# A filter reload queued behind the first stores, and a turned class taken ahead of the products

## The chip, the core and the metric

The kernel runs on one core of a Trainium2 chip. The core has a matrix engine (TensorE, PE in the profile), a vector engine (VectorE, DVE), a scalar engine for pointwise functions (ScalarE, ACT), a general one (GpSimd, POOL) and a sync engine (SyncE, SP). Each follows its own list of instructions in order, and engines wait for one another by semaphores. SP's list consists here of transfers (DMAs): it waits until one may go, issues it and goes on; 16 DMA engines then move the bytes. TensorE writes into a memory of its own, PSUM, which VectorE and ScalarE read out ("evict").

The metric is the device time of one execution in microseconds (us), lower being better.

## What is computed

A global filter over a sequence, then a two-layer network on every token:

```python
X = np.fft.rfft(x, axis=1)                 # x: 8 x 3008 x 256
Y = X * (filt_r + 1j * filt_i)[None]       # filters: 1505 x 256
y = np.fft.irfft(Y, n=x.shape[1], axis=1)
t = y.reshape(8 * 3008, 256)
h = t @ w_in                               # 256 -> 2048
g = h * (1.0 / (1.0 + np.exp(-beta * h)))
out = g @ w_out                            # 2048 -> 256
```

## The kernel before

**The filter of one batch** is a Fourier transform of length 3008 = 47 x 64 made of matrix products, in stages:

- s1 (L613): 16 units, each one product of the input tile xg with table t1 (L619) and one eviction of 96x512 into a tile a1. Four units fill one a1 tile, and the fourth also issues the tile's store to DRAM (d1), L624. Batch 1 takes the odd units' evictions to ScalarE.
- a2_read (L626): four loads (L631) bring d1 back in another layout. The first waits for all four stores.
- s23 (L634): 15 units. Unit i below 12 makes two products (L641) and multiplies them with the filter: VectorE takes p_t from frr (L652) and q_t from fri in two halves (L653, L656), and GpSimd adds them (L657). From unit 3 on there is also the inverse product of unit i - 3 (L667), evicted by ScalarE to z, and every third of these issues a store (L672).
- zz_read and s4 (L674, L682): z is read back and the last product gives y.

The real filter in **frr** is laid out for batches 1 to 7 in 24 slots k. It comes by load_filter (L127): for each third of the slots (8 of 24) four loads of 256 KB, lower (L131) and upper (L134) rows for each of the two halves of the partitions. Slots 8 to 23 of frr hold pieces of w_out until GpSimd has scaled them into wout_sb (L151).

**Batch 0** goes another way, before the network starts, and keeps its result z_t in the chip. It is brought into y in four groups g of eight classes each: turn_z (L532), two per group, is eight transposes (L536) with one eviction by VectorE into a tile zz; last_z (L564), four per group, is four products (L544) and one eviction into y. Group 0 is done before the network starts; groups 1 to 3 run inside it. The evictions of last_z are ScalarE's for groups 1 and 3 and VectorE's for group 2.

**The network** (L812) runs over 47 blocks of 512 tokens and in each over 16 slices of the hidden layer: 752 steps. Step s makes the slice's two hidden products (L825) into hps and ScalarE's activation to gT (L834), then the units that a plan has for this step, then the four output products (L860) of the slice two steps back. After a block's last slice the two halves are evicted to ost tiles and stored (L786, L800).

**The plan** is made by place(a, z, units): it spreads units evenly over steps a to z, and moves one on to the next step where a step already has `per` units. Units of a step stand in the order in which place put them there. The same order holds on every engine, SP's queue among them.

**Pools.** PSUM pool fpsum has three buffers for all these units (L619, L641, L667, L536 and L544); hpsum has two for hps, opsum three for acc. apool has three a1 tiles, the first of which group 0 of batch 0 uses as its zz; so batch 1's a1 tiles 0 and 3 are the same buffer. zzpool has four zz tiles, ostp three ost tiles. A tile's new owner waits until the readers of the old one are done.

**Marks.** L506 is a store of 512 bytes from the last piece of batch 1's input. It stands on SP's queue, so that nothing behind it goes out before that input has landed.

In the listing the lines that the change touches are L520 to L522 (the loads of the first third), uf (L731) and the calls of place from L754 to L768.

Of the kernel before, what the change touches and what calls it, by code (L numbers as in the profile page):

```python
# [24 lines left out]
M = 64  # L25
H = M // 2
NK = 24
J = 32
KG = 6
NG = NK // KG  # L30
JG = 8
# [6 lines left out]
def kernel(  # L38
# [10 lines left out]
    nc = tc.nc  # L49
# [38 lines left out]
    frr = consts.tile([P, NK, D], F32, name="frr", tag="frr")  # L88
# [38 lines left out]
    def load_filter(f_sb, filt, at, k0, n, eng):  # L127
        lo = AP(filt.tensor, filt.offset + k0 * D, [[N1 * D, H], [1, n * D]])
        hi = AP(filt.tensor, filt.offset + (N1 - k0) * D, [[N1 * D, H], [-D, n], [1, D]])
        return [  # L130
            lambda: eng.dma_start(  # L131
                f_sb[at : at + H, k0 : k0 + n, :].rearrange("p k d -> p (k d)"), lo
            ),
            lambda: eng.dma_start(f_sb[at + H : at + M, k0 : k0 + n, :], hi),  # L134
        ]
# [13 lines left out]
    def scale_wout(i):  # L149
        fs = slice(i * WG, (i + 1) * WG)  # L150
        nc.gpsimd.tensor_tensor(  # L151
            wout_sb[:, fs, :],
            staged(i),
            rbeta_sb[:, fs].unsqueeze(2).broadcast_to([P, WG, D]),
            ALU.mult,
        )
# [360 lines left out]

    for i in range(4):
        scale_wout(i)
    for at in (0, M):  # L520
        for go in load_filter(frr, filt_r, at, 0, JG, nc.sync):
            go()  # L522

    ys = {}
    ys[0] = ypool.tile([P, NDC, NK * P], BF16, name="y", tag="y")
# [4 lines left out]
    def turn_z(g, i, on_act=False):  # L530
        if g not in zz0:
            zz0[g] = zzpool.tile([KP, JG, D], BF16, name="zz", tag="zz")  # L532
        pz = fpsum.tile([P, 4, D], BF16, name="pz", tag="f")
        for e in range(4):
            for dc in range(NDC):
                nc.tensor.transpose(  # L536
                    pz[:KP, e, dc * P : (dc + 1) * P], z_t[:, dc, JG * g + 4 * i + e, :], ident[:]
                )
        evac(zz0[g][:, 4 * i : 4 * i + 4, :], pz[:KP], on_act)
# [24 lines left out]
    def last_z(g, i, on_act, own=None):  # L564
        jq, dc = divmod(i, NDC)
        c = g * JG // JC + jq
        yv = ys[0][:, dc, c * CLS : (c + 1) * CLS].rearrange("p (n j) -> p n j", j=JC)

        n0 = NP if jq == 0 else (TB - CLS) // JC
        return last4(zz0[g], t4b, JC * jq, dc, yv, on_act, own, n0)  # L570
# [55 lines left out]
    def a2_read(b):  # L626
        s = st[b]
        s["a2"] = []
        for h in range(NG):
            t = a2pool.tile([P, KG, D], BF16, name="a2", tag="a2")  # L630
            nc.sync.dma_start(t[:], s["d1c"][:, h * KG : (h + 1) * KG, :])  # L631
            s["a2"].append(t)
# [41 lines left out]
    def zz_read(b):  # L674
        s = st[b]
        s["zz"] = []
        for h in range(NJG):
            t = zzpool.tile([KP, JG, D], BF16, name="zz", tag="zz")
            nc.sync.dma_start(t[:], s["d2r"][:, h * JG : (h + 1) * JG, :])
            s["zz"].append(t)  # L680
# [15 lines left out]
    def place(a, z, units, clear=False, per=1):  # L696
        last_at = a
        for n, go in enumerate(units):
            at = a + (z - a) * n / max(1, len(units) - 1)
            at = max(int(at), last_at)  # L700
            if clear and (at % NFB < 2 or at % NFB > 13):
                at += (2 - at) % NFB
            while len(plan.get(at, ())) >= per:
                at += 1
            plan.setdefault(at, []).append(go)
            last_at = at
        return last_at

    def u1(b, act=False):
        def unit(i):  # L710
            def go():
                if i == 0:
                    start(b)
                s1(b, i, act and i % 2 == 1)

            return go

        return [unit(i) for i in range(J // 2)]

    def u23(b):  # L720
        return [lambda i=i: s23(b, i) for i in range(NK // 2 + VLAG)]

    def u4(b, act=False):
        return [lambda i=i: s4(b, i, act and i % 2 == 1) for i in range(J // 2)]

    def uz(g, act=False):
        return [lambda i=i: turn_z(g, i) for i in range(2)] + [
            lambda i=i: last_z(g, i, act) for i in range(2 * NDC)
        ]

    def uf():  # L731
        return [
            go
            for k0 in range(JG, NK, JG)
            for at in (0, M)
            for go in load_filter(frr, filt_r, at, k0, JG, nc.sync)
        ]


    def ut(n):  # L740
        return [
            lambda k=k: nc.vector.tensor_scalar_mul(
                t3[M:P, k : k + NK // n], t3b[M:P, k : k + NK // n], -1.0
            )
            for k in range(0, NK, NK // n)
        ]
# [6 lines left out]

    place(2, 14, uz(1, True))  # L754
    place(15, 29, uz(2))
    place(34, 58, uz(3, True))

    first_step = [(S * b // TB) * NFB for b in range(B + 1)]
    if B > 1:
        units = u1(1, True)  # L760
        place(3, 8, units[: J // 4], per=2)
        at = place(9, 14, units[J // 4 :], per=2)
        place(at + 1, at + 1, [lambda: a2_read(1)] + uf(), per=9)
        place(14, 20, ut(4), per=2)
        at = place(25, 56, u23(1), per=2)
        assert at < 60
        place(60, 60, [lambda: zz_read(1)], per=9)
        place(67, 79, u4(1), per=2)  # L768
    if B > 2:
        place(36, 36, ux(2), per=9)  # L770
        at = place(50, 66, u1(2, True), per=3)
        assert at < 74
        place(74, 74, [lambda: a2_read(2)], per=9)
    for b in range(2, B):
        a = first_step[b - 1]
# [36 lines left out]
    for s in range(len(steps) + LAG):  # L812
# [28 lines left out]
        if s >= LAG:  # L841
# [16 lines left out]
            per = acc[0].shape[1]  # L858
# [48 lines left out]
```

## Time and profile before

| what | before |
| --- | --- |
| time, median of 5 runs (lowest to highest) | 789.58 us (788.66 to 792.14) |
| the profiled execution | 789.58 us, with a span of 787.5 us from the first to the last instruction |
| granted TensorE clock | 1.00 |
| first hidden product of the network | at 35.75 us |
| TensorE busy, 40 to 50 us / 50 to 60 us / 60 to 70 us | 9.89 / 8.25 / 9.95 us |
| TensorE busy, 70 to 80 us / 80 to 90 us / 90 to 100 us | 9.63 / 9.32 / 9.95 us |
| VectorE busy, 60 to 70 us / 70 to 80 us / 80 to 90 us | 6.00 / 9.71 / 9.72 us |
| d<-a, stores of a1 (L624): count, KB, median us to landing | 28, 384, 3.8 |
| a<-d, reads of a2 (L631) | 28, 384, 4.9 |
| frr<-in_filt_r_dram, the filter's loads (L131, L134) | 12, 256, 7.0 |

A row of a timeline has: start in us from the span's start, duration in us, engine, line, operation, output<-input, number; and in brackets how long the engine stood idle before it and who released it. "SPq" is SP issuing a transfer, so its duration is that of the issue and not that of the transfer. Rows of like instructions are merged, so that a row's duration can contain waits between its members. The chain of waits is followed back from the end of the execution: each step is the thing that released the next.

### The profile page before, as it was taken

The page shows a single profiled execution, that of the slowest core. Times are in us where ns is not written, and L with a number is a line of the kernel's source. Part 1 is how long each engine was busy: PE and PEld are TensorE (multiplying, and loading weights), DVE is VectorE, ACT ScalarE, POOL GpSimd, SP SyncE. Part 2 cuts the span into 40 slices and gives each one's busy share as a digit, 9 for nine tenths or more (in the row PEclk, how much of TensorE's full clock was granted, in tenths as well). Part 3 has the DMA queues.
Part 4 walks back from the last instruction along what each step waited for, and adds up shares of the span by engine and source line. Part 5 has one row for each costly group of instructions (what it writes and reads, how often), then busy time and mean ns, then how long its engine had stood idle before and what let it go on. Part 6 is the DMA issues. An engine that isn't in the chain of part 4 may idle for free.

```text
span 787.5 us, 15454 instructions
## 1 busy us (share of the span) xinstructions
PE 771.1 (98%) x6015; PEld 547.8 (70%) x6111; DVE 394.1 (50%) x645; ACT 597.2 (76%) x922; POOL 144.5 (18%) x143
## 2 busy tenths in 40 slices
PE   8999999999999999999999999999999999999997
PEld 5767667766777667876668766686667766776665
DVE  8837835646436564465635746267462761500101
ACT  6977886886678866788677876778767788677776
POOL 8522500420014200231002310024000340000000
PEclk9999999999999999999999999999999999999999
DMA  9978674517801187012850238412370214100101
GB/s 192 250 172 227 161 202 134 126 67 199 223 27 67 52 211 206 28 67 96 200 172 27 95 106 184 151 56 85 112 206 28 75 67 127 49 33 28 55 27 54
DMA packets 84185, 91.46 MB, mean 116 GB/s; under 512 B 4498, under 2 KB 74276, under 8 KB 83154
## 3 DMA queue, kind: packets, MB, share of 16 engines
q1 hardware_dynamic: 81008, 73.95, 30.5%
q0 software_dynamic: 2816, 16.26, 10.6%
q8 instruction: 48, 0.79, 0.4%
q10 hardware_dynamic: 288, 0.26, 0.1%
q14 instruction: 25, 0.20, 0.1%
HBM read 57.16 MB, written 46.66 MB: 132 GB/s over the span
## 4 chain that ended last, share of the span: by engine, by line
PE 90%; DVE 4%; DMA 3%; issue 2%; ACT 1%; DVEq 0%; SPq 0%; ACTq 0%
PE acc L860 41%; PE hps L825 37%; PE ps L619 3%; PE ps L544 3%; PE ps L641 2%; PE ps L667 2%; DMA frr<-in_filt_r_dram 1%; PE pw L187 1%; DVE ost L109 1%; DMA out_dram<-ost 1%; DVE qb_t L444 1%; DMA d<-a 1%; DVE a_t L109 0%; DVE pb_t L444 0%; DVE q_t L656 0%
## 5 line engine op out<-in xcount | busy, mean ns | idle before, releaser
L834 ACT ACTIVATE gT<-hps,beta_sb 128x512 bf16<-128x512 f32 x752 | 516.2, 687 | 175.2 <-PE hps L825 146.9
L860 PE MATMUL acc<-wout_sb,gT 128*128 128x256 bf16 x3008 | 455.1, 272 | 3.8 <-ACT ost L107 0.2
L825 PE MATMUL hps<-y,win_sb 128*128 128x512 bf16 (+8 forms) x1636 | 427.4, 350 | 0.4 <-ACT gT L834 0.3
L860 PEld LDWEIGHTS <-gT 128*128 128x128 bf16 x3008 | 285.4, 98 | 132.3 <-issue 4.3
L825 PEld LDWEIGHTS <-win_sb 128*128 128x128 bf16 x1730 | 164.9, 98 | 24.8 <-issue 0.6
L657 POOL TENSOR_TENSOR v_t<-p_t,q_t 128x512 bf16<-128x512 f32 x84 | 106.6, 1269 | 393.7 <-DVE q_t L656 390.8
L109 DVE COPY ost<-acc 128x512 f32<-128x512 f32 (+1 forms) x88 | 56.2, 678 | 193.6 <-PE acc L860 190.6
L109 DVE CAST a<-ps 96x512 bf16<-96x512 f32 x96 | 65.8, 686 | 90.2 <-PE ps L619 85.3
L111 DVE TENSOR_SCALAR y<-ps 128x376 bf16<-128x376 f32 (+1 forms) x119 | 64.4, 545 | 62.6 <-PE ps L544 62.4
L652 DVE TENSOR_TENSOR p_t<-ps,frr 128x512 f32<-128x512 f32 x84 | 58.1, 692 | 32.0 <-PE ps L641 29.4
L656 DVE TENSOR_TENSOR q_t<-ps,fri 64x512 f32<-64x512 f32 x84 | 58.2, 693 | 1.2
L653 DVE SCALAR_TENSOR_TENSOR q_t<-ps,fri 64x512 f32<-64x512 f32 x84 | 57.4, 684 | 1.1
L544 PEld LDWEIGHTS <-zz 96*128 96x128 bf16 x512 | 35.3, 97 | 30.7 <-issue 2.0
L107 ACT ACTIVATE z<-ps 128x512 bf16<-128x512 f32 x84 | 49.5, 590 | 0.8 <-PE ps L667 0.7
L619 PE MATMUL ps<-xg,t 94*96 94x512 bf16 x112 | 42.0, 381 | 0.7
L544 PE MATMUL ps<-t,zz 96*128 96x94 bf16 x448 | 36.7, 204 | 1.1
L667 PE MATMUL ps<-v_t,t 128*128 128x256 bf16 x168 | 32.1, 273 | 0.6 <-DVE q_t L656 0.6
L641 PE MATMUL ps<-a,t 128*128 128x256 bf16 x168 | 32.1, 273 | 0.4
L118 POOL DMA_DIRECT2D xg<-in_x_dram x22 | 12.0, 550 | 101.0 <-PE acc L860 97.8
L641 PEld LDWEIGHTS <-t 128*128 128x128 bf16 x168 | 15.8, 98 | 14.6
L619 PEld LDWEIGHTS <-t 94*96 94x96 bf16 x112 | 13.8, 123 | 12.1
L667 PEld LDWEIGHTS <-t 128*128 128x128 bf16 x168 | 15.4, 98 | 8.4 <-DVE q_t L656 1.4
(120 smaller groups left out, 195.6 us busy)
## 6 DMA issues: line engine op xcount, KB each, us to landing
out_dram<-ost SPq DMA_DIRECT2D x80, 256.0 KB, 2.1
d<-a SPq DMA_DIRECT2D x28, 384.0 KB, 3.8
a<-d SPq DMA_DIRECT2D x28, 384.0 KB, 4.9
d<-z SPq DMA_DIRECT2D x28, 384.0 KB, 2.3
zz<-d SPq DMA_DIRECT2D x28, 384.0 KB, 6.9
xg<-in_x_dram POOLq DMA_DIRECT2D x6, 1280.0 KB, 10.1
frr<-in_filt_r_dram SPq DMA_DIRECT2D x12, 256.0 KB, 7.0
out_dram<-ost SPq DMA_DIRECT2D x18, 128.0 KB, 2.3
```

Of the source, the lines that this page charges most:

```text
L109: nc.vector.tensor_copy(dst, src)
L111: nc.vector.tensor_scalar_mul(dst, src, scale)
L544: nc.tensor.matmul(ps[:, e, :NP], lhsT=zz[:, jj + e, dc * P : (dc + 1) * P], rhs=tab[:], start=True, stop=True,)
L619: nc.tensor.matmul(ps[:KP], lhsT=t1[:], rhs=s["x"][:, 2 * i : 2 * i + 2, :], start=True, stop=True)
L641: nc.tensor.matmul(ps[:, e, :], lhsT=t2[:, k0 + e, 3:5, :].rearrange("p c k -> p (c k)"), rhs=s["a2"][g][:, kk + e, :], start=True, stop=True,
L652: nc.vector.tensor_tensor(p_t[:], ps[:], frr[:, ks_, :], ALU.mult)
L656: nc.vector.tensor_tensor(q_t[:M], ps[M:P], fri[M:P, ks_, :], ALU.mult)
L657: nc.gpsimd.tensor_tensor(v_t[:], p_t[:], q_t[:], ALU.add)
L667: nc.tensor.matmul(ps[:, e, :], lhsT=t3[:, k0 + e, :], rhs=v_t[:, e, :], start=True, stop=True)
L825: nc.tensor.matmul(hps[:, pos - t0 : pos - t0 + ln], lhsT=win_sb[:, dc, fb * P : (fb + 1) * P], rhs=ys[b][:, dc, n0 : n0 + ln], start=(dc ...
L834: nc.scalar.activation(gT[:, :tn], hps[:, :tn], ACT.Silu, scale=beta_sb[:, fb : fb + 1])
L860: nc.tensor.matmul(acc[tb // per][:, tb % per, :], lhsT=gT[:, tb * P : (tb + 1) * P], rhs=wout_sb[:, fb, :], start=(fb == 0 and tb % per = ...
```

## The change

The four loads of the filter's first third leave their place ahead of the network and become units of step 10, put there after batch 1's s1 units 0 to 7 have been placed. s1's units 8 to 15 may then share a step with more than two units. The two turn_z of group 3 are placed at steps 20 and 24, and its last_z are spread over steps 34 to 58 by themselves.

```diff
     for i in range(4):
         scale_wout(i)
-    for at in (0, M):
-        for go in load_filter(frr, filt_r, at, 0, JG, nc.sync):
-            go()
...
-    def uf():
+    def uf(a, z):
         return [
             go
-            for k0 in range(JG, NK, JG)
+            for k0 in range(a, z, JG)
             for at in (0, M)
             for go in load_filter(frr, filt_r, at, k0, JG, nc.sync)
         ]
...
     place(2, 14, uz(1, True))
     place(15, 29, uz(2))
-    place(34, 58, uz(3, True))
+    units = uz(3, True)
+    place(20, 24, units[:2], per=2)
+    place(34, 58, units[2:])
...
         units = u1(1, True)
         place(3, 8, units[: J // 4], per=2)
-        at = place(9, 14, units[J // 4 :], per=2)
-        place(at + 1, at + 1, [lambda: a2_read(1)] + uf(), per=9)
+        place(10, 10, uf(0, JG), per=9)
+        at = place(9, 14, units[J // 4 :], per=9)
+        place(at + 1, at + 1, [lambda: a2_read(1)] + uf(JG, NK), per=9)
```

What stands where, worked out from the code (steps not named keep their units; nothing changes after step 58):

| unit | step before | step after |
| --- | --- | --- |
| filter's first third, four loads | ahead of step 0 | 10 |
| batch 1's s1 units 9 and 12 | 10 and 12 | 9 and 11 |
| batch 1's other s1 units from 8 on: 8, 10, 11, 13, 14, 15 | 9, 10, 11, 12, 13, 14 | the same |
| group 3's turn_z, 0 and 1 | 34 and 38 | 20 and 24 |
| group 3's last_z, 0 to 3 | 43, 48, 53, 58 | 34, 42, 50, 58 |
| a copy of a fourth of table t3 (VectorE, L742), the last | 20 | 21 |

On SP's queue the order before is: mark, four filter loads, the stores of a1 tiles 0 to 3, the four reads of a2, the eight other filter loads. After it is: mark, the stores of tiles 0 and 1, the four filter loads, the stores of tiles 2 and 3, the reads of a2, the eight other filter loads. fpsum's three buffers go to the units in another order than before from here on.

## The prediction

> **What bounds the kernel now.** The page's busy rows come first: TensorE is busy 98% of the span, ScalarE 76%, VectorE 50%.
>
> ```profile
> PE 771.1 (98%) x6015; PEld 547.8 (70%) x6111; DVE 394.1 (50%) x645; ACT 597.2 (76%) x922; POOL 144.5 (18%) x143
> ```
>
> So the time is TensorE's work plus the places where it stops, and an edit pays only where it shortens a stop. The granted clock is 1.00 in every stretch that I asked for. TensorE's list of waits names nothing between 96 us and the end but one of 0.2 us, so what is lost earlier is not won back later, nor what is gained lost. The stops that the change can touch lie between 45 and 96 us. Ends of matmuls are modelled, so I measure a stop from start to start: a hidden-layer pair (L825) takes 0.43 us of TensorE, an output group of four (L860) 0.44, one s1, L641 or L667 group 0.22, a last_z group 0.17, a turn_z 0.44. These sums give TensorE's timeline to 0.02 us wherever nobody is waited for.
>
> TensorE's timeline at the largest stop:
>
> ```profile
> 52.23 0.59 PE L825 MATMUL hps<-y,win_sb 128*128 128x512 bf16 x2
> 54.53 0.33 PE L544 MATMUL ps<-t4b,zz 96*128 96x94 bf16 x4 [1.70 <-ACT a L107]
> ```
>
> The L544 group was due at 52.23 + 0.435 = 52.66 and began at 54.53: **1.87 us**. It waited for a PSUM buffer of pool fpsum, which ScalarE's eviction of s1's unit 13 was to free. ScalarE's timeline shows what that eviction waited for, and the chain of waits how long the transfer took:
>
> ```profile
> 53.88 0.59 ACT L107 ACTIVATE a<-ps 96x512 bf16<-96x512 f32 x1 [2.50 <-DMA d<-a]
> ```
>
> ```profile
> 47.15 6.63 DMA d<-a
> ```
>
> Unit 13 writes a1's fourth tile. apool has three buffers, so it takes the first tile's and must wait until that one's store (L624) has landed. The SP queue in order of time shows why that is late:
>
> ```profile
> 45.04 0.23 SPq L506 DMA_DIRECT2D mark<-xg  x1
> 45.31 0.31 SPq L131 DMA_DIRECT2D frr<-in_filt_r_dram  x1
> 45.66 0.42 SPq L134 DMA_DIRECT2D frr<-in_filt_r_dram  x1
> 46.13 0.45 SPq L131 DMA_DIRECT2D frr<-in_filt_r_dram  x1
> 46.62 0.42 SPq L134 DMA_DIRECT2D frr<-in_filt_r_dram  x1
> 47.15 9.66 SPq L624 DMA_DIRECT2D d<-a  x4
> 59.72 1.77 SPq L631 DMA_DIRECT2D a<-d  x4
> ```
>
> SP stands at the mark until batch 1's input has landed (45.04). Then come four filter loads, 1.84 us of issue and 1 MB, and only then the first store. Its tile was full at 43.2.
>
> The second place is VectorE between 66 and 91 us, busy without a gap while batch 1's products run. Three stops of TensorE fall there:
>
> ```profile
> 75.81 0.61 PE L536 MATMUL pz<-ident,z_t 128*96 128x128 bf16 x8 [0.27 <-DVE q_t L656]
> ...
> 81.38 0.39 PE L667 MATMUL ps<-v_t,t 128*128 128x256 bf16 x2 [0.39 <-DVE q_t L656]
> ...
> 88.48 0.39 PE L667 MATMUL ps<-v_t,t 128*128 128x256 bf16 x2 [0.23 <-DVE q_t L656]
> ```
>
> From start to start they are 0.43, 0.55 and 0.40 us, and two small ones (93.94 and 95.26) make 0.2 more: 1.59 us. Each is an fpsum buffer that VectorE has not yet read.
>
> **Part 1: the filter's first third.** The four loads move from ahead of all stores to step 10, behind the stores of tiles 0 and 1. They are the same loads, with the same issue time. The first store then goes out at 45.31. The 28 stores L624 take 3.3 to 6.6 us to land, 3.8 in the middle; the fourth, alone on the queue at 56.5, let the reads of L631 go at 59.72, 3.2 us later. So it lands at 48.6 (49.1 by the median). Unit 12 now runs in step 11, at 49.40, and its eviction is wanted at 49.85. In the changed order unit 14 (51.58) needs the buffer that unit 12's VectorE eviction frees; 0.69 us for that says landing by 50.9 costs nothing. Even at 6.6 us (51.9) only 1.0 us would remain. I take the stop as gone: −1.87.
>
> A rule speaks against this. The Trainium skill (DMA: Bandwidth & Descriptors, Bandwidth and the anatomy of one DMA) gives about 2.0 us plus bytes over 436 GB/s. For four loads and one store, 1.44 MB, that is an estimated 5.3 us from 45.31: landed at 50.6, before ScalarE wants the buffer at 51.3, so no stop before and no gain now. The trace has 53.78 for the same bytes, 8.5 us (with two more stores alongside, the queues moved 2.0 MB in these 8.5 us, some 240 GB/s). The row decides: the queue is slower than the rule, and the order in it matters.
>
> What the loads delay instead: SP issues them at about 47.6 to 49.4, before store 2 (tile full at 50.8) and store 3. Unit 15 runs 1.87 earlier, so store 3 goes out at 54.4 instead of 56.5. The bytes ahead of it are those that the trace has through by 55 (195 GB/s in 54 to 55, 19 in the next). So it lands at about 57.7, the reads L631 start some 2 us earlier, and the eight other loads and block 0's output stores behind them on SP as much. Batch 1's products want the reads 1.0 us earlier than before, so slack grows. The first third has 15 us to land before L652 uses it.
>
> The packing of s1 (units 9 and 12 one step earlier) adds no instruction. Steps 9 and 11 hold three fpsum tiles each; unit 9 comes at 46.84 and needs ScalarE's unit 7, done at 46.8; unit 13 comes at 50.49 and needs an eviction done at about 50.4. Bounds 0 and 0.3 (two waits of up to 0.15): I take +0.10.
>
> **Part 2: the turned class.** Two turn_z (eight transposes each, 0.44 us on TensorE, 0.71 on VectorE) go from steps 34 and 38 to 20 and 24, where VectorE waits for TensorE (1.84 us before 64.16, 1.41 before 66.12). TensorE's total is unchanged. Four last_z move up to nine steps earlier; their evictions are ScalarE's, 0.48 us each, and it idles 0.18 to 0.8 us per step there. SP and POOL get nothing from this part. I redo VectorE from the first product: three operations cost 2.12 us, a y eviction 0.58, ost 0.61; 0 is the first L641. Product 3 then ends at 10.05 and product 7 at 19.15. With the buffers that the built program gives, last_z(3,0) takes the old turn's place in step 34, is ready at 9.69 and waits for product 3 as the turn did: 0.42 stays. The stop at 81.38 goes, since that buffer is now product 4's, done at 12.2 when wanted at 14.4. The third becomes a wait for product 7: ready at 18.92, so 0.29. With 0.1 for the small ones, 0.81 is left of 1.59: −0.78. The same reckoning on the old order gives all three old stops at their places. Without that cover (the old stops all stay) the part is worth 0; the most is −1.59.
>
> **Sum.** −1.87 + 0.10 − 0.78 = −2.55 us. The profiled execution took 789.58 us with a span of 787.5, and 789.58 is also the median of the five runs: 787.03, so **787.0 us**, −0.32%.
>
> **The rivals.**
> 1. *Only the SP part pays.* VectorE remains saturated and the first turned stop stays by my own count; another eviction takes the rest. −1.87 + 0.1: 787.8. For it: VectorE still has 25.1 us of work in a stretch of some 26. Against: the buffers do differ.
> 2. *The stop changes its name.* The store lands no sooner than the rows of stores under load (6.6), or steps 9 to 12 wait for evictions: 1.0 stays, 0.3 is added, and TensorE reaches the products with half of part 2's gain: −0.87 + 0.3 − 0.4 = −1.0: 788.6. Against: nothing is ahead of the store on its queue.
> 3. *Slower: batch 1's reads come late.* Stores 2 and 3 now queue behind 1 MB. The first product is wanted at 64.7 and the first read needs 3.3, so store 3 must land by 61.4; it has 3.7 us beyond my 57.7. It must be over 6.2 us late to undo the gain. The filter loads themselves land up to 9.5 us after issue with 2 MB and reads in front: for store 3 that is 63.9, 2.5 past the limit, which just cancels the gain. The slowest transfer into that tile (w_out's pieces, at 27 us with every queue full) took 15.7: 70.1, 8.7 past. I price it halfway, at 12.6: 67.0, 5.6 past, 5.6 - 2.55 = +3.1: 792.6. Block 0's output stores, next on SP, would hold VectorE's ost too. Against: at 54.4 the queue is nearly drained in the trace.
>
> **How the numbers follow.** A measurement of this kernel can tell 0.3%, 2.37 us, from no change (its own runs spread 788.66 to 792.14). My forecast has 0.58, with 0.5 us of doubt either way, so about three quarters of it pass the bound; rival 1 has 0.20 and a tenth passes; rival 2 0.11, rival 3 0.07, unnamed 0.04, half of it slower. Faster 0.48, same 0.43, slower 0.09. The range runs from 786.2 (part 2 at its most, −1.59) to 788.9 (rival 2 and some spread).
>
> **What would show it.** Right: in the SP queue two L624 issues straight after the mark; no start of TensorE late by over 0.3 us between 50 and 55; L631 issued near 57.7; a stop of about 0.4 at step 34, none at step 38. Wrong: a DMA named before an s1 eviction near 50, a wait for a<-d or frr at the first L641 or L652, or new stops at step 20 or 24.

## The result, and the profile after

The changed kernel takes **787.07 us** (median of 21 runs, 786.87 to 788.32) against 789.51 us of the kernel before (41 runs beside it). The ratio is 0.997 with a 95% interval of 0.9963 to 0.9976, and the forecast was 787.0. The profiled execution has a span of 785.0 us.

TensorE did the same work; what went is time in which it stood. The page's busy row, for comparison with 771.1 of before:

```profile
PE 770.8 (98%) x6015; PEld 548.0 (70%) x6111; DVE 393.9 (50%) x645; ACT 597.1 (76%) x922; POOL 144.5 (18%) x143
```

From L523 to the calls of place the lines of the kernel after are three lower than before: the stores of a1 are L621 now, the reads L628, the eviction to p_t L649. First SP's queue, in order of time, with the same columns as in the prediction:

```profile
44.66 0.23 SPq L506 DMA_DIRECT2D mark<-xg  x1
45.00 2.14 SPq L621 DMA_DIRECT2D d<-a  x2
47.19 0.53 SPq L131 DMA_DIRECT2D frr<-in_filt_r_dram  x1
47.77 0.56 SPq L134 DMA_DIRECT2D frr<-in_filt_r_dram  x1
48.37 1.42 SPq L131 DMA_DIRECT2D frr<-in_filt_r_dram  x1
49.83 0.42 SPq L134 DMA_DIRECT2D frr<-in_filt_r_dram  x1
50.84 3.96 SPq L621 DMA_DIRECT2D d<-a  x2
57.69 1.78 SPq L628 DMA_DIRECT2D a<-d  x4
```

The first store goes out right behind the mark, at 45.00, and lands 3.1 us later, where it took 6.63. The reads start at 57.69 instead of 59.72. TensorE at step 14:

```profile
52.24 0.59 PE L825 MATMUL hps<-y,win_sb 128*128 128x512 bf16 x2
52.67 0.33 PE L541 MATMUL ps<-t4b,zz 96*128 96x94 bf16 x4
```

The group that stood until 54.53 now starts 0.43 us after the pair before it: nothing is waited for. In VectorE's stretch two stops are left, at steps 34 and 42 (TensorE's timeline):

```profile
74.85 0.33 PE L541 MATMUL ps<-t4b,zz 96*128 96x94 bf16 x4 [0.48 <-DVE q_t L653]
...
84.08 0.39 PE L664 MATMUL ps<-v_t,t 128*128 128x256 bf16 x2 [0.25 <-DVE q_t L653]
```

They were due at 74.43 and 83.66, so each is 0.42 us long.

To compare executions step by step I line them up at the network's first output group (L860), since the network's start varies by up to 1 us from one execution to the next. The table gives the start of the n-th output group after the first, in us from the first (TensorE's timeline). The last three columns are experiments 1, 2 and 3:

| n, output group of step | before | after | loads alone | turn alone | own buffer |
| --- | --- | --- | --- | --- | --- |
| 11, step 13 | 13.80 | 13.79 | 13.79 | 13.79 | 13.79 |
| 12, step 14 | 16.91 | 15.05 | 15.05 | 16.55 | 15.05 |
| 74, step 76 | 86.68 | 84.16 | 84.81 | 85.97 | 84.80 |

The changed kernel is 1.86 us ahead at step 14 and 2.52 at step 76, and the spans differ by 2.5. So the whole gain is made by step 76, and none of it is given back.

### The profile page after: what moved, and what is told of

Read it like the earlier page. It is cut to its first block, busy times and chain, and to the rows that moved or that the text cites. A ratio compares the mean times of both kernels' runs of the same rounds, so it can differ in the third digit from the quotient of the medians.

```text
span 785.0 us, 15454 instructions
## 1 busy us (share of the span) xinstructions
PE 770.8 (98%) x6015; PEld 548.0 (70%) x6111; DVE 393.9 (50%) x645; ACT 597.1 (76%) x922; POOL 144.5 (18%) x143
## 4 chain that ended last, share of the span: by engine, by line
PE 93%; DVE 3%; issue 2%; ACT 0%; DVEq 0%; ACTq 0%
PE acc L860 42%; PE hps L825 38%; PE ps L616 3%; PE ps L541 3%; PE ps L638 2%; PE ps L664 2%; PE pw L187 1%; DVE ost L109 1%; DVE qb_t L444 1%; DVE a_t L109 0%; DVE pb_t L444 0%; PE pz L533 0%; DVE q_t L653 0%; DVE q_t L650 0%; ACT z_t L107 0%
## 5 line engine op out<-in xcount | busy, mean ns | idle before, releaser
L860 PE MATMUL acc<-wout_sb,gT 128*128 128x256 bf16 x3008 | 455.0, 272 | 3.8 <-ACT ost L107 0.2
L860 PEld LDWEIGHTS <-gT 128*128 128x128 bf16 x3008 | 285.5, 98 | 132.5 <-issue 4.2
L649 DVE TENSOR_TENSOR p_t<-ps,frr 128x512 f32<-128x512 f32 x84 | 58.1, 692 | 30.9 <-PE ps L638 28.5
```

Of the source, the lines that this page charges most:

```text
L649: nc.vector.tensor_tensor(p_t[:], ps[:], frr[:, ks_, :], ALU.mult)
L860: nc.tensor.matmul(acc[tb // per][:, tb % per, :], lhsT=gT[:, tb * P : (tb + 1) * P], rhs=wout_sb[:, fb, :], start=(fb == 0 and tb % per = ...
```

## The experiments

Times are medians with the interval of the ratio to the kernel before, run beside each.

**1. The loads alone.** Group 3 stays where it was.

```diff
-    units = uz(3, True)
-    place(20, 24, units[:2], per=2)
-    place(34, 58, units[2:])
+    place(34, 58, uz(3, True))
```

> The first part alone: the filter loads move, group 3's turned class stays at steps 34 to 58. Theory (two separate stops): the stop of 1.87 us at step 14 is gone and the three VectorE stops (0.43, 0.55, 0.40) return at steps 34, 38 and 44, so about 1.8 us under before and 0.7 over the full change: 787.8. Rival (one part carries it all, VectorE's stretch gives nothing): 787.1, the same as the full change.

787.89 us (9 runs; 0.9962 to 0.9984). TensorE's timeline has no stop at step 14, and the old three are all back:

```profile
74.05 0.61 PE L533 MATMUL pz<-ident,z_t 128*96 128x128 bf16 x8 [0.26 <-DVE q_t L653]
...
79.62 0.39 PE L664 MATMUL ps<-v_t,t 128*128 128x256 bf16 x2 [0.39 <-DVE q_t L653]
...
86.72 0.39 PE L664 MATMUL ps<-v_t,t 128*128 128x256 bf16 x2 [0.23 <-DVE q_t L653]
```

86.68 - 84.81 = 1.87 us of the gain are the loads' (last row of the table), and on top of them the turned class is worth 84.81 - 84.16 = 0.65. That is read from one profile of each kernel; the intervals of the two medians overlap. The theory stands; that one part carries everything is out.

**2. The turned class alone.** The three lines the other way round, put into the kernel before.

> The second part alone: the turned class moves, the loads stay ahead of the stores. Theory: the stop of 1.87 us before 54.53 stays, the VectorE stretch has stops of about 0.4 at steps 34 and 42 and none at 38, so 0.7 us under before: 788.8. Rival (the two parts need each other, or the second gives nothing): 789.5.

788.83 us (13 runs; 0.9983 to 1.0: not told apart from before by these runs). TensorE's timeline:

```profile
54.62 0.33 PE L544 MATMUL ps<-t4b,zz 96*128 96x94 bf16 x4 [1.34 <-ACT a L107]
...
76.79 0.33 PE L544 MATMUL ps<-t4b,zz 96*128 96x94 bf16 x4 [0.47 <-DVE q_t L656]
...
86.02 0.39 PE L667 MATMUL ps<-v_t,t 128*128 128x256 bf16 x2 [0.26 <-DVE q_t L656]
...
95.12 0.39 PE L619 MATMUL ps<-xg,t 94*96 94x512 bf16 x1 [0.28 <-ACT ost L107]
```

The stop at step 14 stays and VectorE's are those of the changed kernel. The table has this kernel 0.71 ahead of before, but not all of that is the part's. In this execution the first store landed 6.3 us after its issue and not 6.6, and the stop at step 14 was 0.36 shorter. From step 14 to step 76 the part gains only 0.35 (69.77 before, 69.42 now), because a new stop of 0.45 stands at 95.12, in front of the first s1 unit of batch 2.

The row names ScalarE's ost, which ends at that moment. The unit also reads batch 2's input xg, and the rows of that tile fit better:

```profile
L118 POOL DMA_DIRECT2D xg<-in_x_dram x2: 512/552/591, 83.1 to 83.7; - x2
...
DMA to landing us min/median/max: 10.5/10.9/11.3
```

(The numbers of the first line are min, median and max ns of an issue, then the first and the last start.) The second load goes out at 83.7 and takes 11.3 us. Four profiles side by side:

| kernel | second load of xg goes out | takes | landed | the unit begins |
| --- | --- | --- | --- | --- |
| turned class alone | 83.7 | 11.3 | 95.0 | 95.12 |
| changed kernel | 81.7 | 10.9 | 92.6 | 92.77 |
| changed kernel again (experiment 9) | 81.8 | 11.1 | 92.9 | 93.06 |
| s1 not packed (experiment 4) | 81.7 | 11.2 | 92.9 | 93.04 |

Each time the unit begins 0.1 to 0.2 us after the landing. So the turned class brings TensorE to a place where the next batch's input limits it, and how much of the part's gain is seen hangs on when that load lands: 0.35 here, 0.65 on top of the loads.

**3. A buffer of its own for tile 3.** The kernel before, with the loads ahead of the stores.

```diff
-            s["a1"] = apool.tile([KP, JG, D], BF16, name="a1", tag="a1")
+            own = b == 1 and g == 3
+            s["a1"] = (zzpool if own else apool).tile(
+                [KP, JG, D], BF16, name="a1", tag="zz" if own else "a1"
+            )
```

> Before, but batch 1's a1 tile 3 gets a buffer of its own from the zz pool; the loads stay ahead of the stores and the turned class where it was. Theory (the stop is nothing but the wait of tile 3 for tile 0's store): the first store still lands some 6.6 us after its issue, and the stop is gone all the same: 787.7, like the loads alone. Rival (the late stores hurt in another way too, by late reads or the SP queue): less than 1.0 us gained, or a new wait for a<-d at the first L641.

787.53 us (9 runs; 0.9967 to 0.9986), 1.88 ahead of before in the table. The first store, seen in the rows of its line, is as late as before, 6.5 us after an issue at 46.83:

```profile
L627 SPq DMA_DIRECT2D d<-a x2: 383/426/468, 46.8 to 47.3; - x2
...
DMA to landing us min/median/max: 6.5/6.5/6.5
```

A late store for whose buffer nobody waits cost nothing here. So the cause is the reuse of the buffer, and the order of the queue is one of two cures.

**4. s1 not packed.** The changed kernel with two units a step again; the loads stand last in step 10.

```diff
-        place(10, 10, uf(0, JG), per=9)
-        at = place(9, 14, units[J // 4 :], per=9)
+        at = place(9, 14, units[J // 4 :], per=2)
+        place(10, 10, uf(0, JG), per=9)
```

> The full change, but s1's units 9 and 12 stay in steps 10 and 12, two units a step; the loads stand at the end of step 10. Theory (the packing costs and gains nothing): within 0.2 us of the full change, 787.1. Rival (the packing frees the loads or the stores earlier, or costs up to 0.3): 0.3 us off either way, seen as a stop between 46 and 53.

787.24 us (10 runs; 0.9965 to 0.9984). Lined up, it is at 15.05 at step 14, as the changed kernel is, and 0.18 behind at step 76. This arises at batch 2's first s1 unit:

```profile
93.04 0.39 PE L616 MATMUL ps<-xg,t 94*96 94x512 bf16 x1
```

Its input landed at 92.9 (the table of experiment 2), and the changed kernel's second execution lost 0.1 at the same place, so this is not the packing's. The packing itself is worth 0.00.

**5 and 6. Half of the loads ahead.** First the lower rows stay ahead of the first store, then the upper ones (the number swaps).

```diff
+    for at in (0, M):
+        load_filter(frr, filt_r, at, 0, JG, nc.sync)[0]()
...
-        place(10, 10, uf(0, JG), per=9)
+        place(10, 10, uf(0, JG)[1::2], per=9)
```

> The full change, but the two loads of the lower rows (L131, long contiguous rows) stay ahead of the first store; the two of the upper rows (L134, rows of 1 KB in falling order) move. Theory (bytes and issue time ahead in the queue set the landing, half of them are left): the first store issues near 46.0 and lands near 50.5 to 51.2, so a stop of 0 to 0.3: 787.1 to 787.4. Rival (the upper rows are the slow ones): it lands by 49.5 and there is no stop.

> The full change, but the two loads of the upper rows (L134) stay ahead of the first store and those of the lower rows move. Theory (bytes and issue time): the same as with the lower rows ahead, a stop of 0 to 0.3, 787.1 to 787.4. Rival (the upper rows are the slow ones): the store lands at 52.5 or later and a stop of 0.6 to 1.3 us stays at the unit of step 13 or 14: 787.7 to 788.4.

787.80 us (19 runs; 0.9973 to 0.9988) and 787.57 us (22 runs; 0.9968 to 0.9985). VectorE's timeline has the eviction of unit 12 waiting for the store; with the lower rows ahead:

```profile
52.60 0.69 DVE L109 CAST a<-ps 96x512 bf16<-96x512 f32 x1 [2.55 <-DMA d<-a]
```

and with the upper rows ahead:

```profile
51.44 0.69 DVE L109 CAST a<-ps 96x512 bf16<-96x512 f32 x1 [2.25 <-DMA d<-a]
```

Such an eviction starts 0.12 us after the landing (53.78 to 53.90 in the kernel before), so the stores landed at 52.48 and 51.32. From the mark that is 7.1 and 5.7 us, between 8.7 with all four loads ahead and 3.4 with none. TensorE stops 0.75 and 0.44 us. With half of the bytes ahead the store lands between the two, but the middle, which I had expected for both, holds for neither: in these two profiles it lands later behind the lower rows, the opposite of the rival.

More than that isn't shown. It is one profile of each, and the other two loads, those behind the first store, go out at 48.22 and 47.84, while it is still under way, so they can have held it back too. Both variants also have runs (786.91 and 786.95) as short as the shortest of the changed kernel (786.87), which leaves hardly any room there for a stop of this length.

**7. All of the filter behind the reads.**

```diff
-        place(10, 10, uf(0, JG), per=9)
...
-        place(at + 1, at + 1, [lambda: a2_read(1)] + uf(JG, NK), per=9)
+        place(at + 1, at + 1, [lambda: a2_read(1)] + uf(0, NK), per=13)
```

> The full change, but the filter's first third goes out only behind the reads of a2, ahead of the other two thirds. Theory (from there its transfer takes the 8 us that the first loads behind the reads took): the stores land earlier and the reads start up to 1 us earlier, but the first third is there only near 68, some 3 us after VectorE wants it at 65.2; VectorE has no slack behind it, so 2.5 to 3.5 us over the full change: 789.6 to 790.6, a wait for frr at L652. Rival (the last loads start early enough, or VectorE catches up): within 0.5 us of the full change.

793.21 us (6 runs; ratio 1.005, 1.0036 to 1.0064), 6.1 over the changed kernel and twice what I expected. VectorE's first product (VectorE's timeline), and then TensorE's:

```profile
71.28 0.69 DVE L649 TENSOR_TENSOR p_t<-ps,frr 128x512 f32<-128x512 f32 x1 [6.17 <-DMA frr<-in_filt_r_dram]
```

```profile
73.44 0.50 PE L541 MATMUL ps<-t4b,zz 96*128 96x94 bf16 x4 [4.10 <-DVE q_t L653]
```

Two terms were off. The first third of the filter was there at 71.2 and not near 68: its four loads went out from 59.86 to 61.7, and I had taken the 7.9 us of one load for all four. And TensorE's clock fell. In the table of stretches (stretch in us, its length, busy us and instructions of TensorE, weight loads, VectorE, ScalarE and GpSimd, then granted clock, DMA share, GB/s):

```profile
70.00:72.00 2.00, 0.00 (x0) 0.00 (x0) 0.70 (x2) 0.12 (x1) 0.00 (x0) 1.00 1.07 221
72.00:74.00 2.00, 0.50 (x4) 0.37 (x5) 1.92 (x4) 0.00 (x0) 0.54 (x1) 0.63 1.10 223
74.00:76.00 2.00, 1.99 (x8) 1.17 (x8) 1.97 (x3) 0.00 (x0) 0.72 (x1) 0.50 1.11 221
76.00:78.00 2.00, 2.00 (x8) 1.06 (x7) 1.93 (x4) 0.69 (x1) 1.27 (x1) 0.50 1.01 205
78.00:80.00 2.00, 2.00 (x13) 1.35 (x11) 1.94 (x4) 1.28 (x2) 1.13 (x1) 0.66 0.90 263
```

Lined up, 4.8 us are lost by the output group right behind the stop and 2.3 more in the seven groups after that (10.3 us, where the changed kernel takes 8.0). So there is a latest place for the first third: step 10 is early enough, step 15 is too late.

**8. Group 2's evictions on ScalarE.** The changed kernel, with one line more changed:

```diff
-    place(15, 29, uz(2))
+    place(15, 29, uz(2, True))
```

> The full change, and group 2's four last_z evictions go to ScalarE. Theory (what is left at steps 34 and 42 is VectorE's lag, to which two evictions of 0.58 us each in this stretch add): product 3 ends 1.15 us earlier, both stops of 0.42 go, 0.8 us under the full change: 786.2. Rival (ScalarE, busier by the four evictions, is late with its activations, or the buffers fall otherwise): no gain, 787.1, with waits for ACT gT at L825 between 60 and 72.

786.66 us (5 runs; 0.9949 to 0.9977), and 0.48 ahead of the changed kernel at step 76, not 0.8. The two stops that VectorE made are gone but for 0.08, and just behind the first another has come up. In step 34 TensorE's output groups (TensorE's timeline) contain a gap, the fourth weight load is late (that of weight loads), and ScalarE (its own) shows why:

```profile
74.64 0.88 PE L860 MATMUL acc<-wout_sb,gT 128*128 128x256 bf16 x4
```

```profile
75.15 0.10 PEld L860 LDWEIGHTS <-gT 128*128 128x128 bf16 x1 [0.29 <-issue]
```

```profile
74.02 0.59 ACT L107 ACTIVATE z<-ps 128x512 bf16<-128x512 f32 x1
74.49 0.60 ACT L107 ACTIVATE ost<-acc 128x512 f32<-128x512 f32 x1
```

The new block's second acc tile takes the buffer of the old block's first half, and ScalarE's ost reads that until 75.09, having stood behind z. These rows name no releaser, but the times fit to 0.06 us, and in experiment 10, where the same wait stands at the head of its row, the row names ost. While TensorE came 0.42 late itself, this cost nothing.

**9. The same beside the changed kernel, on one chip.**

> The changed kernel once more, as the standard for the run beside it on the same chip. Expected at 787.1 and 2.5 us under before, with two stops of 0.42 at steps 34 and 42.

> The full change with group 2's evictions on ScalarE, once more and beside the full change on one chip. Theory (one stop of 0.42 and 0.35 of the other go, a wait of 0.28 for ScalarE's ost comes up behind the first): 0.5 us under the full change, 786.6. Rival (the difference seen before is that of two chips or of two executions): the same time as the full change within 0.2 us.

787.26 us (5 runs; 0.9952 to 0.9977) and 786.56 us (5 runs; 0.9942 to 0.9969). The intervals overlap; lined up at step 76 the profiles are 84.27 and 83.69. So this version is ahead of the changed kernel by the medians of two runs and by the place of the stops in two profiles, by 0.4 to 0.7 us, though the intervals don't tell the two apart.

**10. Only the turns moved.** The changed kernel, with group 3's last_z at their old steps.

```diff
-    place(34, 58, units[2:])
+    place(43, 58, units[2:])
```

> The full change, but group 3's four last_z keep their old steps 43, 48, 53 and 58; only its two turn_z move. Theory (what is left is VectorE's lag, and it shows wherever TensorE next asks for a buffer that VectorE still reads): no stop at steps 34 and 42, since nothing is asked for there that is late, but one of some 0.8 at step 44, where the inverse product takes product 8's buffer: 787.1, within 0.2 of the full change. Rival (the stop at step 34 belongs to last_z's place and is lost for good with it): 0.4 to 0.8 us under the full change, 786.3 to 786.7.

787.86 us (9 runs; 0.997 to 0.9989). The stop at step 44 is where it was reckoned, and one at step 34 comes on top (TensorE's timeline):

```profile
75.22 0.38 PE L860 MATMUL acc<-wout_sb,gT 128*128 128x256 bf16 x2 [0.29 <-ACT ost L107]
...
86.35 0.39 PE L664 MATMUL ps<-v_t,t 128*128 128x256 bf16 x2 [0.37 <-DVE q_t L653]
```

Nothing stops at step 42 and TensorE stands for product 8 at step 44, 0.53 us instead of 0.8. I had expected no stop at step 34: with last_z gone from it, the wait for ScalarE's ost is bare, as in experiment 8. The kernel is 0.26 behind the changed one at step 76, just outside what I gave it. The stop that was moved came back where the next buffer was wanted.

**11. Products one step earlier**, on top of experiment 8.

```diff
-        at = place(25, 56, u23(1), per=2)
+        at = place(24, 55, u23(1), per=2)
```

> As the run with group 2's evictions on ScalarE, and batch 1's products spread over steps 24 to 55 instead of 25 to 56, so that product 4 and its z eviction leave step 33, where ScalarE evicts block 1's first half. Theory (the 0.28 that came up at step 34 is the output group's wait for that eviction, which stood behind z): it goes, with 0.08 at step 42: 0.3 us under that run, 786.3. Rival (the first product, one step earlier, meets the turn_z of the same step or the reads and the filter, or another wait takes the place): no gain or up to 0.5 us lost.

787.66 us (14 runs, 786.55 to 795.34; 0.997 to 1.0): no gain over experiment 8. The profiled execution, of 795.34, is one that stood for a store of z. TensorE's timeline, and then ScalarE's:

```profile
94.15 1.01 PE L825 MATMUL hps<-y,win_sb 128*128 128x512 bf16 x2 [5.80 <-ACT gT L834]
```

```profile
92.92 0.60 ACT L107 ACTIVATE z<-ps 128x512 bf16<-128x512 f32 x1 [6.47 <-DMA d<-z]
```

The chain of waits has that store:

```profile
79.52 13.32 DMA d<-z
```

The other 13 runs take at most 788.47, so this profile can't tell whether the 0.28 was saved. That stays open, and so does why the store took 13.32 us.

## Why the prediction was right

- **The stop at step 14** (-1.87 forecast): gone, 1.86 measured by the lined-up start of step 14. The cause was reckoned rightly and experiment 3 shows it: no queue was moved there, and the stop went with the buffer's reuse. The first store landed 3.1 us after its issue; 3.3 had been taken.
- **The rule against the row.** The rule's 5.3 us would have had no stop before and no gain. The row, 8.5 us, decided rightly; half the loads ahead still left stops of 0.75 and 0.44, which the rule's price doesn't have either. But the page that the prediction names gives its fit for one transfer issued by GpSimd. Using it for five on SP's queue was the prediction's own step, so the row doesn't refute the page.
- **What the loads delay.** Reads at 57.69 against 57.7 forecast, the first product's group at 64.74 against 64.7. Rival 3 did not come: neither the reads nor the filter were late for the first product. Experiment 7, with the loads 5 steps further on, makes what it feared.
- **The packing** (+0.10): 0.00, by experiment 4.
- **The turned class** (-0.78): 0.65 on top of the loads, 0.13 less than forecast. The stop at step 34 is 0.42 as reckoned, that at step 38 is gone. The one at step 42 was put at 0.29 and is 0.42, and that is the whole difference. The term that was off is the ost eviction, 0.61 in my sum. VectorE's timeline has it at 76.95, and the next product begins 0.72 later; product 7 so ends at 84.02, 19.28 after the first group, where I had 19.15:

```profile
76.95 0.69 DVE L109 COPY ost<-acc 128x512 f32<-128x512 f32 x1
77.67 0.69 DVE L649 TENSOR_TENSOR p_t<-ps,frr 128x512 f32<-128x512 f32 x1
...
83.33 0.69 DVE L653 TENSOR_TENSOR q_t<-ps,fri 64x512 f32<-64x512 f32 x1
```

- **The sum**: -2.55 forecast, -2.52 lined up, -2.44 in the medians. Two terms were off, the packing (0.10 too dear) and the turned class (0.13 too good), and they nearly cancel. That the sum comes so close is in this part luck. So is the profiled execution of the changed kernel, in which batch 2's input came almost in time; in its second execution it cost 0.1.
- **Rival 1** would have had 787.8, and that is what the loads alone take (787.89). **Rival 2** did not come: SP's first store had nothing ahead of it but the mark. That a store which lands late leaves a part of the stop is seen in experiments 5 and 6.

## What to carry to other kernels

Ask of a late wait which reuse makes it, not only which transfer: the same stop went by the order of the queue and by one more buffer. When an engine works without a gap, follow which PSUM buffer each consumer takes and when its last reader ends; this gave the changed kernel's two stops by VectorE to within 0.15 us. It gave 0.8 for 0.53 in experiment 10, and it missed the waits that lay hidden behind these stops: for ScalarE's ost, and for the next batch's input. Before counting on a stop's removal, look for the next wait within its length: 0.28 of 0.42 us was behind it here.

## What was unexpected in the hardware

**A long stop costs more than itself.** In experiment 7 the granted clock was 1.00 until TensorE had stood some 3 us, then 0.50 until about 79, and the groups after the stop took 2.3 us longer. In the execution of experiment 11 that stood 5.8 us it was the same (table of stretches, columns as above):

```profile
90.00:92.00 2.00, 0.00 (x0) 0.00 (x0) 0.00 (x0) 0.00 (x0) 0.00 (x0) 0.92 0.48 139
92.00:94.00 2.00, 0.00 (x0) 0.00 (x0) 0.00 (x0) 1.08 (x3) 0.00 (x0) 0.50 0.33 129
...
98.00:100.00 2.00, 2.00 (x15) 1.39 (x14) 0.63 (x1) 1.36 (x3) 1.21 (x1) 0.87 0.00 0
```

The moments follow from the means. A stretch of 2 us with a mean of 0.63 had 0.52 us at full clock and the rest at half, so the clock fell at 72.5 and, with 0.66 in the last row of experiment 7, was back at 79.4. In experiment 11 it fell at 91.7 and was back at 98.5. Both times it was half for 6.8 us. The 1.87 us stop of the kernel before left the clock at 1.00.

The Trainium skill (TensorE: Matmul & The Clock Gate, Part 1) says that the array falls to half rate after an idle window of about 3.4 us and comes back after about as long a busy one. The fall agrees: stops of 4.1 and 5.8 us, as the profile names the waits, halve the clock, and 1.87 us does not. The return was slower: work resumed at 73.44 and 94.15, 5.9 and 4.4 us before full clock. My price for experiment 7 lacked all of this.

**Equal bytes ahead, different landings.** Behind two loads of 256 KB in long contiguous rows the first store landed 7.1 us after the mark, behind two of the same size in rows of 1 KB 5.7. These are one profile each, and the loads behind the store differ too, so whether the shape does it stays open.
